# One-core decode block: the loads issued by GpSimd as single packets in place of SyncE's loads

## The chip, the core and the metric

The kernel runs on one core of a Trainium2 chip. The metric is device time in microseconds (us), the median of three runs. TensorE (PE) does the matmuls, VectorE (DVE) and ScalarE (ACT) the elementwise work, GpSimd (POOL) and SyncE (SP) little besides constants and transfers. Transfers between the chip's memory (DRAM) and the on-chip buffer run on the core's 16 DMA engines, whichever engine issues them.

## The reference

One token of width 640 goes through an attention block with a cached context and then a gated feed-forward block:

```python
B, Sq, D = 1, 1, 640
H, Sk, Dh = 32, 8192, 192
q = (layernorm(x) @ wq) per head
scores = einsum("bhqd,bhkd->bhqk", q, k_cache) * (Dh ** -0.5)
o = einsum("bhqk,bhkd->bhqd", softmax(scores), v_cache)
h = x + o @ wo
gate, up = layernorm(h) @ W_gate, layernorm(h) @ W_up      # F = 1536
out = h + (relu(gate) * up) @ W_down
```

All data are float32. Keys and values of 32 heads, 8192 positions and 192 features each are 403 MB; with the weights some 446 MB have to be read once.

## The kernel before

The host packs the inputs into matrices of 128 rows, one row for each partition, in the order in which they are used. The on-chip buffer holds three slots of 128 x 16320 floats, `slot_x`, `slot_y` and `slot_z` (`X`, `Y`, `Z` in the code). A load fills (most of) a slot: 128 rows of up to 65,280 bytes, one for each partition, eight for each DMA engine.

Heads are worked on in units (`pe_unit`): scores of one head from its keys (`pe_k`, L180), the values of the head before it (`pe_v`, L187), and the query and output projections on VectorE (`dve_d1`, `dve_wo`). A loop of `NTURN` = 10 turns handles three heads a turn. Each turn has five loads, `row_1` to `row_5`: `row_1` into X, `row_2` into Z, `row_3` into Y, `row_4` into X, `row_5` into Y. Ahead of the loop `row_p` goes into Y; behind it come the last head and the feed-forward weights in eleven smaller loads with `row_p` (`row_t1`, `row_t2a`, `row_t2b`, `row_t3`, `row_up`, `row_gate`, four pieces of `row_down`). That makes 61 loads.

Two families of semaphores set the order. `land[n]` (and `tl[...]` behind the loop) rises to 16 when load n has landed; PE and DVE wait for it. `free[n]` tells that the consumers are done with the part of a slot that load n filled; the issuer waits for it, takes 16 off `land[n]`, and issues the next load into that slot. `free[5]`, for instance, is set by DVE when its last instruction of `dve_wo` (L377) on `woc` in Y is done, and `row_3` goes into Y on that. In the kernel before all this is SP's program (`sync_program`); GpSimd's program (`pool_program`) writes a few constants at the start (`ones`, `pat`, `ident`) and is then done. At the end `fout` tells that the output `o4` is written; SP and ACT each store one half, and SP waits for both (`out_s`, `out_a`).

The kernel reserves 2048 bytes of each partition for descriptors of transfers that GpSimd issues (`dynamic_dma_scratch_size`); before the change nothing uses them.

Of the kernel before, what the change touches and what calls it, by code (L numbers as in the profile page):

```python
# [8 lines left out]
ET = mybir.EngineType  # L9

P, D, H, S, DH, F = 128, 640, 32, 8192, 192, 1536
# [7 lines left out]
NTURN = (H - 2) // 3  # L19
SCALE = DH ** -0.5  # L20
EPS = 1e-5
DG, FG = D // 4, F // 4

W_P = 14272
# [61 lines left out]
def build(nc, arrays):  # L86
# [31 lines left out]
    o4 = sb("o4", [P, DG])  # L118
# [14 lines left out]
    def wait(eng, s, n, sub=0, **kw):  # L133
        w = eng.wait_ge(s, n)  # L134
        if sub:
            w.then_inc(s, -sub)
        return w
# [37 lines left out]
    te = nc.tensor  # L175
# [37 lines left out]
    def pe_unit(kblk, vblk, rows, freed=None, freed_at=None, q_next=True):  # L213
        def landed(n):
            if n in rows:
                s, sub = rows[n]
                wait(te, s, 16, sub)

        wait(te, a2p, 1, 1)
        landed("k0")  # L220
        pe_k(kblk, 0)
        wait(te, a2p, 1, 1)
        pe_o()
        wait(te, a2p, 1, 1)
        pe_l()
        landed("k1")
        pe_k(kblk, 1)
        landed("v0")
        at = None if freed is None else (freed_at, freed)
        pe_v(vblk, 0, 8, inc_at=at)  # L230
        landed("v8")
        pe_v(vblk, 8, 24, inc_at=at)
        if q_next:
            wait(te, d2p, 2, 2)
            if freed is not None and freed_at < 24 and freed is not fin:
                te.sem_inc(freed, 1)
            pe_q()
        else:
            wait(te, d2p, 1, 1)
        pe_t()  # L240
        landed("v24")
        pe_v(vblk, 24, 32, last=p2a)

    def tensor_program():
        wait(te, cst_pe, 1, 1)
        wait(te, pre, 1, 1)
        op(te.matmul(pl[:, 0:1], ones, vec["s1"], start=True, stop=True), inc=p2d)
        wait(te, pre, 1, 1)
        op(te.matmul(pl[:, 0:1], ones, vec["s2"], start=True, stop=True), inc=p2d)
        wait(te, d2p, 1, 1)  # L250
        pe_q()
        wait(te, a2p, 1, 1)
        wait(te, land[5], 16)
        pe_k(kp, 0)
        pe_k(kp, 1)
        wait(te, d2p, 2, 2)
        pe_q()
        pe_t()
        with te.Fori(0, NTURN):
            pe_unit(ka, va, {"k0": (land[1], 0), "v8": (land[2], 0)}, free[1], 7)  # L260
            pe_unit(kb, vb, {"k1": (land[3], 0), "v24": (land[4], 0)}, free[3], 23)
            pe_unit(kc, vcc, {"v0": (land[5], 0)})
        pe_unit(kt, vt, {"k0": (tl["t1"], 16), "v8": (tl["t2a"], 16)}, fin, 7, q_next=False)
        wait(te, a2p, 1, 1)
        pe_o()
        wait(te, a2p, 1, 1)
        pe_l()
        wait(te, tl["t2b"], 16, 16)
        pe_v(vz, 0, 16)
        wait(te, d2p, 3, 3)  # L270
        for g in range(4):
            te.matmul(acc[Q(g), 0:DG], ones[Q(g), 0:32], xd[Q(g)].rearrange("p c j -> p (c j)"),
                      start=True, stop=False, tile_position=(32 * g, 32 * g))
        for g in range(4):
            te.matmul(acc[Q(g), 0:DG], ones[:, 0:32], accs[:, g * DG:(g + 1) * DG], start=False, stop=False)
        for g in range(4):
            r = slice(0, 64) if g < 2 else slice(64, P)
            te.matmul(acc[Q(g), 0:DG], ones[r, 0:32], accs[r, D + (g % 2) * DG:D + (g % 2 + 1) * DG],
                      start=False, stop=False)
        wait(te, tl["t3"], 16, 16)  # L280
        pe_v(vz, 16, 32, last=p2a)
        wait(te, a2p, 1, 1)
        pe_o()
        wait(te, d2p, 1, 1)
        for g in range(4):
            te.matmul(acc[Q(g), 0:DG], oc[:, 0:1].to_broadcast([P, 32]), woz[:, g * DG:(g + 1) * DG],
                      start=False, stop=False)
        for g in range(4):
            r = slice(0, 64) if g < 2 else slice(64, P)
            m = te.matmul(acc[Q(g), 0:DG], oc[r, 1:2].to_broadcast([64, 32]),  # L290
                          woz[r, D + (g % 2) * DG:D + (g % 2 + 1) * DG], start=False, stop=True)
        m.then_inc(p2a, 1)
        wait(te, a2p, 1, 1)
        op(te.matmul(pt[:, 0:1], ones, vec["hs1"], start=True, stop=True), inc=p2d)
        wait(te, d2p, 1, 1)
        op(te.matmul(od[:, 0:1], ones, vec["hs2"], start=True, stop=True), inc=p2d)
        wait(te, tl["up"], 16, 16)
        for j in range(DJ):
            for g in range(4):
                m = te.matmul(sc[Q(g), 0:FG], hc[:, j, :], up[:, j, g * FG:(g + 1) * FG],  # L300
                              start=(j == 0), stop=(j == DJ - 1))
        op(m, inc=p2a)
        wait(te, tl["gate"], 16, 16)
        for j in range(DJ):
            for g in range(4):
                m = te.matmul(sc[Q(g), 512:512 + FG], hc[:, j, :], gate[:, j, g * FG:(g + 1) * FG],
                              start=(j == 0), stop=(j == DJ - 1))
        op(m, inc=p2d)
        wait(te, d2p, 1, 1)
        wait(te, tl["d0"], 16, 16)  # L310
        for j in range(FJ):
            if j == 6:
                wait(te, tl["d1"], 16, 16)
            if j == 10:
                wait(te, tl["d2"], 16, 16)
            if j < FJ - 1:
                for g in range(4):
                    te.matmul(q_ps[Q(g), 0:DG], guT[:, j, :], down[:, j * D + g * DG:j * D + (g + 1) * DG],  # L318
                              start=(j == 0), stop=False)
            else:  # L320
                for half in range(2):
                    if half:
                        wait(te, tl["d3"], 16, 16)
                    for g in range(2 * half, 2 * half + 2):
                        m = te.matmul(q_ps[Q(g), 0:DG], guT[:, j, :], down[:, j * D + g * DG:j * D + (g + 1) * DG],  # L325
                                      start=False, stop=True)
        op(m, inc=p2d)
# [199 lines left out]
        po_.sem_inc(cst_pe, 1)  # L527
        po_.sem_inc(cst_ve, 1)

    sp = nc.sync  # L530

    def load(t, src, s):
        sp.dma_start(t, src).then_inc(s, 16)

    def sync_program():
        load(Y[:, 0:W_P], dram["row_p"], land[5])
        r1, r2, r3, r4, r5 = (dram[f"row_{i}"] for i in range(1, 6))
        load(X[:, 0:W_1], r1[0], land[1])
        load(Z[:, 0:W_2], r2[0], land[2])

        def turn(i):
            wait(sp, free[5], 1, 1)
            wait(sp, land[5], 16, 16)
            load(Y[:, 0:W_3], r3[i], land[3])
            wait(sp, free[1], 2, 2)
            wait(sp, land[1], 16, 16)
            load(X[:, 0:W_4], r4[i], land[4])
            wait(sp, free[3], 2, 2)
            wait(sp, land[3], 16, 16)
            load(Y[:, 0:W_5], r5[i], land[5])  # L550
            wait(sp, free[2], 1, 1)
            wait(sp, land[2], 16, 16)
            wait(sp, free[4], 1, 1)
            wait(sp, land[4], 16, 16)

        with sp.Fori(0, NTURN - 1) as i:
            turn(i)
            load(X[:, 0:W_1], r1[i + 1], land[1])
            load(Z[:, 0:W_2], r2[i + 1], land[2])
        turn(NTURN - 1)  # L560
        load(X[:, 0:W_T1], dram["row_t1"], tl["t1"])
        load(Z[:, 0:W_T2A], dram["row_t2a"], tl["t2a"])
        load(Z[:, W_T2A:W_T2A + W_T2B], dram["row_t2b"], tl["t2b"])
        wait(sp, free[5], 1, 1)
        wait(sp, land[5], 16, 16)
        load(Y[:, 0:W_T3], dram["row_t3"], tl["t3"])
        load(Y[:, W_T3:W_T3 + W_UP], dram["row_up"], tl["up"])
        wait(sp, fin, 1, 1)
        load(X[:, 0:W_UP], dram["row_gate"], tl["gate"])
        for n, (a, b) in enumerate(DOWN):  # L570
            load(X[:, W_UP + a:W_UP + b], dram["row_down"][:, a:b], tl[f"d{n}"])
        wait(sp, fout, 1)
        load(out[0, 0, 0:D // 2].rearrange("(g n) -> g n", g=2), o4[31:33, :], out_s)
        wait(sp, out_s, 16, 16)
        wait(sp, out_a, 16, 16)
        wait(sp, fout, 1, 1)

    programs = ((ET.PE, tensor_program), (ET.DVE, vector_program), (ET.Activation, scalar_program),
                (ET.Pool, pool_program), (ET.SP, sync_program))
    for e, _ in programs:  # L580
        nc.br(f"prog_{e.name}", engines=[e])
    for e, f in programs:
# [12 lines left out]
```

## Time and profile before

| | us |
|---|---|
| median of 3 runs | 1039.3 (1038.07 to 1039.48) |
| the profiled execution's own time | 1039.63 |
| its span, first to last instruction | 1038.3 |
| PE busy | 547.4 (53%) |
| DVE busy | 188.2 (18%) |
| POOL busy | 1.2 |
| time that the packets of SP's queue took, share of 16 engines | 99.4% |

The profile comes from one execution, 0.3 us above the median; 1.3 us of it lie outside the span. Busy shares of engines are averages over the span. The DMA share is the mean over the 16 DMA engines; a packet in the table of queues is one transfer of one engine as the profiler records it. An issue (SPq) is the instruction with which an engine starts a load; its time to landing runs from there to the last byte's semaphore.

### The profile page before, as it was taken

How to read it: one execution, taken by the hardware profiler on the slowest of the kernel's cores; microseconds unless marked ns; L12 is line 12 of the kernel's file. 1: busy time of each engine (PE TensorE's matmuls, PEld its weight loads, DVE VectorE, ACT ScalarE, POOL GpSimd, SP SyncE). 2: the span in 40 equal slices, each digit the busy share in tenths (PEclk: the TensorE clock that was granted, in tenths of full speed). 3: DMA queues.
4: the chain of work that ended last, by engine and by line, in shares of the span. 5: the costliest groups of instructions: out<-in, count | busy, mean ns of one | idle time of the engine just before them, and what ended most of it. 6: DMA issues, size and time to landing. Idle time of an engine off the chain costs nothing. (4 is left out here: it accounts for less than half of the span.)

```text
span 1038.3 us, 10306 instructions
## 1 busy us (share of the span) xinstructions
PE 547.4 (53%) x4492; PEld 176.3 (17%) x4492; DVE 188.2 (18%) x478; ACT 41.2 (4%) x137; POOL 1.2 (0%) x11
## 2 busy tenths in 40 slices
PE   0746446456363563654544546536465463564676
PEld 0211112112121120111111112112111121121123
DVE  1211221112122021221121220212221121220111
ACT  1000000000000000000000000000000000000010
POOL 0000000000000000000000000000000000000000
PEclk9876867768677677776787867867877778687787
DMA  9999999999999999999999999999999999999997
GB/s 402 441 432 425 434 435 431 445 420 435 435 439 433 425 438 436 440 427 432 435 435 426 433 438 431 444 426 433 433 438 438 420 438 436 438 432 425 432 427 326
DMA packets 8800, 446.07 MB, mean 430 GB/s; under 512 B 980, under 2 KB 1112, under 8 KB 1240
## 3 DMA queue, kind: packets, MB, share of 16 engines
q1 hardware_dynamic: 8788, 445.94, 99.4%
q8 instruction: 7, 0.11, 0.0%
q14 instruction: 1, 0.01, 0.0%
q10 hardware_dynamic: 4, 0.00, 0.0%
HBM read 445.94 MB, written 0.00 MB: 429 GB/s over the span
## 5 line engine op out<-in xcount | busy, mean ns | idle before, releaser
L180 PE MATMUL sc<-slot_x,qs 128*32 128x512 f32 x1008 | 150.9, 743 | 109.6 <-DMA slot_x<-row 99.9
L187 PE MATMUL po<-slot_y,p 128*2 128x384 f32 x1152 | 117.9, 562 | 80.2 <-DMA slot_y<-row 77.4
L187 PE MATMUL po<-slot_z,p 128*2 128x384 f32 x560 | 72.5, 671 | 91.7 <-DMA slot_z<-row 88.4
L180 PE MATMUL sc<-slot_y,qs 128*32 128x512 f32 x288 | 54.1, 913 | 83.0 <-DMA slot_y<-row 82.5
L187 PE MATMUL po<-slot_x,p 128*2 128x384 f32 x336 | 43.6, 651 | 86.1 <-DMA slot_x<-row 86.1
L373 DVE COPY oc<-od 128x2 f32<-128x2 f32 x32 | 5.1, 159 | 389.5 <-PE od L206 389.5
L385 DVE STREAM_TRANSPOSE st<-sc 128x512 f32<-128x512 f32 x64 | 45.7, 714 | 164.4 <-PE sc L180 164.4
L180 PEld LDWEIGHTS sc<-slot_x,qs 128*32 128x32 f32 x1008 | 35.4, 134 | 200.8 <-DMA slot_x<-row 106.3
L187 PEld LDWEIGHTS po<-slot_y,p 128*2 128x2 f32 x1152 | 29.1, 94 | 167.7 <-DMA slot_y<-row 86.5
L391 DVE TENSOR_REDUCE m<-pt 128x1 f32<-128x128 f32 x32 | 9.3, 292 | 162.6 <-PE pt L199 162.6
L187 PEld LDWEIGHTS po<-slot_z,p 128*2 128x2 f32 x560 | 15.0, 102 | 138.3 <-DMA slot_z<-row 95.6
L474 ACT COPY qs<-q_ps 128x96 f32<-128x96 f32 x32 | 7.7, 239 | 766.9 <-ACTq L134 766.9
L367 DVE SCALAR_TENSOR_TENSOR prod<-slot_y,xn,prod 128x192 f32<-128x192 f32 x88 | 36.9, 419 | 3.1
L180 PEld LDWEIGHTS sc<-slot_y,qs 128*32 128x32 f32 x288 | 11.4, 154 | 113.8 <-DMA slot_y<-row 83.4
L180 PE MATMUL sc<-slot_z,qs 128*32 128x512 f32 x240 | 27.6, 592 | 0.0
L187 PEld LDWEIGHTS po<-slot_x,p 128*2 128x2 f32 x336 | 8.6, 94 | 109.5 <-DMA slot_x<-row 88.0
L203 PEld LDWEIGHTS od<-mrl,ob 128*128 128x128 f32 x132 | 18.1, 199 | 34.2 <-issue 34.2
L478 ACT COPY ob<-po 128x384 f32<-128x384 f32 x32 | 15.3, 479 | 181.1 <-ACTq L134 181.1
L203 PE MATMUL od<-mrl,ob 128*128 128x1 f32 x132 | 20.8, 262 | 1.6 <-PEq L134 1.6
L194 PE MATMUL q_ps<-pat,prod 128*128 128x96 f32 x64 | 15.4, 323 | 8.5 <-PEq L134 8.5
L365 DVE TENSOR_SCALAR prod<-slot_y,xn 128x192 f32<-128x192 f32 x22 | 6.9, 315 | 65.4 <-DMA slot_y<-row 65.3
L376 DVE SCALAR_TENSOR_TENSOR accs<-slot_y,oc,accs 128x640 f32<-128x640 f32 x21 | 18.5, 879 | 0.0
(95 smaller groups left out, 248.6 us busy)
## 6 DMA issues: line engine op xcount, KB each, us to landing
slot_x<-row SPq DMA_DIRECT2D x10, 8160.0 KB, 26.9
slot_z<-row SPq DMA_DIRECT2D x10, 8160.0 KB, 45.8
slot_y<-row SPq DMA_DIRECT2D x10, 8160.0 KB, 24.7
slot_x<-row SPq DMA_DIRECT2D x10, 7680.0 KB, 35.6
slot_y<-row SPq DMA_DIRECT2D x10, 7584.0 KB, 27.1
slot_x<-row_t SPq DMA_DIRECT2D x1, 7680.0 KB, 25.2
slot_y<-row_p SPq DMA_DIRECT2D x1, 7136.0 KB, 19.6
slot_z<-row_t2a SPq DMA_DIRECT2D x1, 5088.0 KB, 36.9
```

The costliest lines, as they stand in the source:

```text
L180: m = te.matmul(sc[Q(g), half * 512:half * 512 + 512], qs[:, 32 * part:32 * part + 32], blk(half, part * 4 + g), start=(part == 0), stop=( ...
L187: m = te.matmul(po[32 * g:32 * g + 2, 0:PW], p[:, 2 * i:2 * i + 2], blk(i), start=(i < 4), stop=(i >= 28))
L194: te.matmul(q_ps[:, 0:96], prod[:, 0:P], pat[:, 0, :], start=True, stop=False)
L203: te.matmul(od[:, 0:1], ob[:, k * DH:k * DH + P], mrl[:, k:k + 1], start=(k == 0), stop=(k == 1))
L365: dv(ve.tensor_scalar(prod, w3[:, 0, :], xn[:, 0:1], None, op0=ALU.mult), w=first)
L367: dv(STT(prod, w3[:, j, :], xn[:, j:j + 1], prod, op0=ALU.mult, op1=ALU.add), w="self", inc=d2p if j == DJ - 1 else None)
L373: dv(ve.tensor_copy(oc, od[:, 0:2]), w=pd())
L376: dv(STT(accs[:, 0:D], w[:, 0:D], oc[:, 0:1], accs[:, 0:D], op0=ALU.mult, op1=ALU.add), w="self", inc=inc)
L385: return dv(ve.transpose(st[:, s], sc[:, s]), w=w)
L391: dv(ve.reduce_max(vec["m1"], pt[:, 0:P], axis=AX.X, negate=True), w=pd(), inc=d2a)
L474: op(ac.copy(qs, q_ps[:, 0:96]), inc=a2p)
L478: op(ac.copy(ob, po[:, 0:PW]), inc=a2p)
```

## The change

All 61 loads move from SP's program to GpSimd's. Each is issued with `single_packet`, which asks the software that writes GpSimd's descriptors to mark all of one engine's rows of a load as one packet. Where SP took 16 off a landing semaphore as part of its wait, GpSimd now waits and then runs an instruction of its own (`inc_swdge_sem`, mode "sub"), which keeps its books on its queue as well. PE therefore no longer takes 16 off the `tl` semaphores behind the loop; GpSimd does that at the very end, ten times, and only then sets `fin`, for which SP waits behind the two stores. GpSimd's constants are written behind its first three loads. SP keeps the store of its half of the output.

```diff
+SINGLE = True
...
-        wait(te, tl["t2b"], 16, 16)
+        wait(te, tl["t2b"], 16)
...
-    def load(t, src, s):
-        sp.dma_start(t, src).then_inc(s, 16)
-
-    def sync_program():
+    def load(t, src, s, **kw):
+        po_.dma_start(t, src, single_packet=SINGLE, **kw).then_inc(s, 16)
+
+    def settled(s):
+        wait(po_, s, 16)
+        po_.inc_swdge_sem([s], [16], mode="sub")
+
+    def load_program():
         load(Y[:, 0:W_P], dram["row_p"], land[5])
...
         load(X[:, 0:W_1], r1[0], land[1])
         load(Z[:, 0:W_2], r2[0], land[2])
+        pool_program()
 
         def turn(i):
-            wait(sp, free[5], 1, 1)
-            wait(sp, land[5], 16, 16)
+            wait(po_, free[5], 1, 1)
+            settled(land[5])
             load(Y[:, 0:W_3], r3[i], land[3])
...
-        with sp.Fori(0, NTURN - 1) as i:
+        with po_.Fori(0, NTURN - 1) as i:
             turn(i)
...
+        wait(po_, fout, 1)
+        for s in tl.values():
+            settled(s)
+        po_.sem_inc(fin, 1)
+
+    sp = nc.sync
+
+    def sync_program():
         wait(sp, fout, 1)
-        load(out[0, 0, 0:D // 2].rearrange("(g n) -> g n", g=2), o4[31:33, :], out_s)
+        sp.dma_start(out[0, 0, 0:D // 2].rearrange("(g n) -> g n", g=2), o4[31:33, :]).then_inc(out_s, 16)
         wait(sp, out_s, 16, 16)
         wait(sp, out_a, 16, 16)
+        wait(sp, fin, 1, 1)
         wait(sp, fout, 1, 1)
```

The first place is the loop. These are the rows of SP in one turn before (an ISA row is the wait and the computing of the address; the names in brackets are the semaphores waited for):

```order
L533 ISA [waits free5,land5]
L533 DMA slot_y<-row 128x16320
L533 ISA [waits free1,land1]
L533 DMA slot_x<-row 128x15360
L533 ISA [waits free3,land3]
L533 DMA slot_y<-row 128x15168
L533 ISA [waits free2,land2,free4,land4]
L533 DMA slot_x<-row 128x16320
L533 DMA slot_z<-row 128x16320
```

And these are the rows of POOL in one turn of the change, L536 being the instruction that takes 16 off and L532 the address and the load:

```order
L536 ISA [waits free5,land5]
L532 ISA
L532 DMA slot_y<-row 128x16320
L536 ISA [waits free1,land1]
L532 ISA
L532 DMA slot_x<-row 128x15360
L536 ISA [waits free3,land3]
L532 ISA
L532 DMA slot_y<-row 128x15168
L536 ISA [waits free2,land2]
L536 ISA [waits free4,land4]
```

Every load now has one or two more instructions between its wait and its issue, all on POOL's queue; the waits themselves and the order of the loads are the same.

The second place is the end of POOL's program, from the last load on (before, POOL has nothing there):

```order
L532 DMA slot_x<-row_down 128x320
L536 ISA [waits tl_t1,fout]
L536 ISA [waits tl_t2a]
L536 ISA [waits tl_t2b]
L536 ISA [waits tl_t3]
L536 ISA [waits tl_up]
L536 ISA [waits tl_gate]
L536 ISA [waits tl_d0]
L536 ISA [waits tl_d1]
L536 ISA [waits tl_d2]
L536 ISA [waits tl_d3]
```

Ten instructions come behind `fout`, beside the store of the output, and SP, behind its wait for the two stores, now waits for the end of them.

## Rows read from the trace of the kernel before

**Rows 1.** The page's first part: busy time, share of span, instructions.
```profile
span 1038.3 us, 10306 instructions
PE 547.4 (53%) x4492; PEld 176.3 (17%) x4492; DVE 188.2 (18%) x478; ACT 41.2 (4%) x137; POOL 1.2 (0%) x11
```

**Rows 2.** The page's DMA totals, and its queues (packets, MB, share of 16 engines).
```profile
DMA packets 8800, 446.07 MB, mean 430 GB/s; under 512 B 980, under 2 KB 1112, under 8 KB 1240
...
q1 hardware_dynamic: 8788, 445.94, 99.4%
q8 instruction: 7, 0.11, 0.0%
```

**Rows 3.** Who waited for whom: engine, line, releaser: total us, times, longest.
```profile
PE sc L180 <- DMA slot_x<-row: 99.9, 9, 11.5
...
PE po L187 <- DMA slot_z<-row: 88.4, 10, 9.4
...
PE po L187 <- DMA slot_x<-row: 86.1, 10, 9.1
...
PE sc L180 <- DMA slot_y<-row: 82.5, 10, 8.7
PE po L187 <- DMA slot_y<-row: 77.4, 10, 8.2
```

**Rows 4.** Rates by stretch: us, busy of each engine, PEclk, DMA share, GB/s.
```profile
100.00:900.00 800.00, 419.95 (x3407) 131.47 (x3399) 146.24 (x363) 28.62 (x103) 0.00 (x0) 0.76 1.00 433
...
1005.00:1022.00 17.00, 12.24 (x96) 4.79 (x100) 2.27 (x11) 1.08 (x4) 0.00 (x0) 0.63 1.01 432
...
1026.50:1030.00 3.50, 3.50 (x29) 1.41 (x21) 0.00 (x0) 0.00 (x0) 0.00 (x0) 0.51 1.01 426
```

**Rows 5.** DMA issues of the page: count, KB each, median us to landing.
```profile
slot_x<-row SPq DMA_DIRECT2D x10, 8160.0 KB, 26.9
slot_z<-row SPq DMA_DIRECT2D x10, 8160.0 KB, 45.8
slot_y<-row SPq DMA_DIRECT2D x10, 8160.0 KB, 24.7
slot_x<-row SPq DMA_DIRECT2D x10, 7680.0 KB, 35.6
slot_y<-row SPq DMA_DIRECT2D x10, 7584.0 KB, 27.1
...
slot_y<-row_p SPq DMA_DIRECT2D x1, 7136.0 KB, 19.6
```

**Rows 6.** The first turn's `row_3`, alone, by the same view.
```profile
slot_y<-row SPq DMA_DIRECT2D x1, 8160.0 KB, 23.7
```

**Rows 7.** Timeline of the start: start us, us, engine, line, operation.
```profile
0.31 0.10 POOL L590 MEMSET const-float32-0.0<- 128x1 f32 x1 [0.31 <-issue]
...
0.41 0.10 POOL L590 MEMSET const-uint8-127<- 128x1 uint8 x1
0.81 0.42 SPq L533 DMA_DIRECT2D slot_y<-row_p  x1
...
1.36 0.29 POOL L522 TENSOR_SCALAR_AFFINE_SELECT ident<-ones 128x128 f32<-128x128 f32 x1
...
1.60 0.25 POOL L525 MEMSET pat<- 128x16 f32 x4
```

**Rows 8.** Timeline of the second turn around the issue of `row_3`.
```profile
146.71 0.88 DVE L376 SCALAR_TENSOR_TENSOR accs<-slot_y,oc,accs 128x640 f32<-128x640 f32 x1
147.51 0.55 DVE L377 SCALAR_TENSOR_TENSOR accs<-slot_y,oc,accs 128x320 f32<-128x320 f32 x1
148.43 0.33 SPq L533 DMA_DIRECT2D slot_y<-row  x1
...
154.22 3.38 PE L187 MATMUL po<-slot_z,p 128*2 128x384 f32 x20 [9.26 <-DMA slot_z<-row]
```

**Rows 9.** Timeline of the end.
```profile
1026.02 5.13 PE L306 MATMUL sc<-slot_x,hc 128*32 128x384 f32 x40 [2.42 <-PEq L134]
...
1036.47 0.38 DVE L467 SCALAR_TENSOR_TENSOR o<-q_ps,hr,h 128x160 f32<-128x160 f32 x1 [3.83 <-PE q_ps L325]
1036.88 0.34 SPq L533 DMA_DIRECT2D out<-o  x1
```

**Rows 10.** The queues in the stretch of 2 us from 102 to 104.
```profile
q8 instruction: 1, 0.02, 3.2%
```

More of the change, by code (lines that the diff above doesn't have):

```diff
@@ L262, in tensor_program @@
             pe_unit(kc, vcc, {"v0": (land[5], 0)})
-        pe_unit(kt, vt, {"k0": (tl["t1"], 16), "v8": (tl["t2a"], 16)}, fin, 7, q_next=False)
+        pe_unit(kt, vt, {"k0": (tl["t1"], 0), "v8": (tl["t2a"], 0)}, fin, 7, q_next=False)
         wait(te, a2p, 1, 1)
@@ L279, in tensor_program @@
                       start=False, stop=False)
-        wait(te, tl["t3"], 16, 16)
+        wait(te, tl["t3"], 16)
         pe_v(vz, 16, 32, last=p2a)
@@ L296, in tensor_program @@
         op(te.matmul(od[:, 0:1], ones, vec["hs2"], start=True, stop=True), inc=p2d)
-        wait(te, tl["up"], 16, 16)
+        wait(te, tl["up"], 16)
         for j in range(DJ):
@@ L302, in tensor_program @@
         op(m, inc=p2a)
-        wait(te, tl["gate"], 16, 16)
+        wait(te, tl["gate"], 16)
         for j in range(DJ):
@@ L309, in tensor_program @@
         wait(te, d2p, 1, 1)
-        wait(te, tl["d0"], 16, 16)
+        wait(te, tl["d0"], 16)
         for j in range(FJ):
             if j == 6:
-                wait(te, tl["d1"], 16, 16)
+                wait(te, tl["d1"], 16)
             if j == 10:
-                wait(te, tl["d2"], 16, 16)
+                wait(te, tl["d2"], 16)
             if j < FJ - 1:
@@ L322, in tensor_program @@
                     if half:
-                        wait(te, tl["d3"], 16, 16)
+                        wait(te, tl["d3"], 16)
                     for g in range(2 * half, 2 * half + 2):
@@ L528, in pool_program @@
         po_.sem_inc(cst_ve, 1)
-    sp = nc.sync
-    def load(t, src, s):
-        sp.dma_start(t, src).then_inc(s, 16)
-    def sync_program():
+    def load(t, src, s, **kw):
[4 more added lines that the diff above has]
+    def load_program():
+        r1, r2, r3, r4, r5 = (dram[f"row_{i}"] for i in range(1, 6))
         load(Y[:, 0:W_P], dram["row_p"], land[5])
-        r1, r2, r3, r4, r5 = (dram[f"row_{i}"] for i in range(1, 6))
         load(X[:, 0:W_1], r1[0], land[1])
         load(Z[:, 0:W_2], r2[0], land[2])
+        pool_program()
         def turn(i):
-            wait(sp, free[5], 1, 1)
-            wait(sp, land[5], 16, 16)
+            wait(po_, free[5], 1, 1)
+            settled(land[5])
             load(Y[:, 0:W_3], r3[i], land[3])
-            wait(sp, free[1], 2, 2)
-            wait(sp, land[1], 16, 16)
+            wait(po_, free[1], 2, 2)
+            settled(land[1])
             load(X[:, 0:W_4], r4[i], land[4])
-            wait(sp, free[3], 2, 2)
-            wait(sp, land[3], 16, 16)
+            wait(po_, free[3], 2, 2)
+            settled(land[3])
             load(Y[:, 0:W_5], r5[i], land[5])
[L551 to L554, printed above, removed]
-        with sp.Fori(0, NTURN - 1) as i:
+            wait(po_, free[2], 1, 1)
+            settled(land[2])
+            wait(po_, free[4], 1, 1)
+            settled(land[4])
+        with po_.Fori(0, NTURN - 1) as i:
             turn(i)
@@ L563, in sync_program @@
         load(Z[:, W_T2A:W_T2A + W_T2B], dram["row_t2b"], tl["t2b"])
-        wait(sp, free[5], 1, 1)
-        wait(sp, land[5], 16, 16)
+        wait(po_, free[5], 1, 1)
+        settled(land[5])
         load(Y[:, 0:W_T3], dram["row_t3"], tl["t3"])
         load(Y[:, W_T3:W_T3 + W_UP], dram["row_up"], tl["up"])
-        wait(sp, fin, 1, 1)
+        wait(po_, fin, 1, 1)
         load(X[:, 0:W_UP], dram["row_gate"], tl["gate"])
@@ L571, in sync_program @@
             load(X[:, W_UP + a:W_UP + b], dram["row_down"][:, a:b], tl[f"d{n}"])
+        wait(po_, fout, 1)
[4 more added lines that the diff above has]
+    def sync_program():
         wait(sp, fout, 1)
-        load(out[0, 0, 0:D // 2].rearrange("(g n) -> g n", g=2), o4[31:33, :], out_s)
+        sp.dma_start(out[0, 0, 0:D // 2].rearrange("(g n) -> g n", g=2), o4[31:33, :]).then_inc(out_s, 16)
         wait(sp, out_s, 16, 16)
         wait(sp, out_a, 16, 16)
+        wait(sp, fin, 1, 1)
         wait(sp, fout, 1, 1)
     programs = ((ET.PE, tensor_program), (ET.DVE, vector_program), (ET.Activation, scalar_program),
-                (ET.Pool, pool_program), (ET.SP, sync_program))
+                (ET.Pool, load_program), (ET.SP, sync_program))
     for e, _ in programs:
```

## The prediction

> **What bounds the kernel now.** I read the page's engine shares first: no compute engine is busy for much more than half of the span, and POOL for 1.2 us [rows 1]. The transfers fill it instead: the packets of SP's queue take 99.4% of 16 engines' time, 446 MB in all [rows 2]. The waits say the same from the other side: ten times each, PE stands idle some 8 to 10 us for one of the five loads of a turn [rows 3]. So PE, DVE and ACT could all be somewhat later or earlier and nothing would change; the end moves with the last bytes. Next, the rate. Between 100 and 900 us, 433 GB/s flow at a DMA share of 1.00 [rows 4]. At that rate 446 MB take 1030 us; some 2 to 3 us lie ahead of the first bytes and 3 to 5 behind the last, and 1.3 outside the span.
>
> Whether a load is issued early enough is read from its time to landing less its own transfer. A load of 8160 KB is 8.36 MB, 19.3 us at 433 GB/s. The three such loads land 26.9, 45.8 and 24.7 us after their issue, the other two (7680 and 7584 KB, 18.2 and 17.9 us) after 35.6 and 27.1 [rows 5]. So they are issued 7.6, 26.5, 5.4, 17.4 and 9.2 us ahead of the moment at which their own bytes could start. The thinnest cover is that of `row_3`: 5.4 us in the median, 23.7 - 19.3 = 4.4 us in the first turn [rows 6]. The timeline shows its chain: DVE ends `dve_wo` at 148.06, SP issues at 148.43, and PE sees the load ahead of it, `row_2`, land at 154.22 [rows 8].
>
> **The change, part by part.**
>
> *The start.* SP issues `row_p` at 0.81 with an instruction of 0.42 us [rows 7]. It lands 19.6 us later, though 7.31 MB take 16.9 us at 433 GB/s, so 2.7 us are latency and ramp [rows 5, 4]. Nothing hides this. GpSimd's issue replaces SP's, and no row shows how long its software needs for a load. Lower end: no longer than SP, 0.42 us. Upper end: POOL starts its shortest instructions every 0.034 us (four from 0.31 to 0.41, [rows 7]); if each of the 128 rows of a load cost that much, 4.4 us. The ends lie a factor of ten apart and neither row is like it, so I take the geometric middle, 1.4 us, and so +1.0 us (0 to +4.0). The Trainium skill ("DMA: Bandwidth & Descriptors", Specifications) gives about 1 us to the first byte on GpSimd's path and 0.6 on SP's; no trace here has yet shown GpSimd's. By it this term would be +0.4, an estimate from that page, and the sum 0.6 lower. The constants behind the first three loads are wanted only when `row_p` has landed, some 20 us in, so they cost nothing; if they came later than that, they would count in full.
>
> *The stream.* Each of the 50 loads of the loop gets one or two instructions more between wait and issue, and the longer issue: +0.05 to +0.11 us for each taking of 16 (as much as POOL's short instructions, [rows 7]) and +1.0 us. What hides it is the load still under way. `row_3`, with 5.4 us of cover, needs at most the 2.7 us of latency that the first load shows; 2.7 us are left (1.7 in the first turn), against 1.2 wanted. So 0. If the cover goes, each microsecond too much is lost ten times. What is queued behind a late `row_3` on POOL are `row_4` and `row_5`, with 17.4 and 9.2 us of cover, so they follow without harm. The Trainium skill ("SBUF — State Buffer", SBUF: two separate sides) warns against just this: while VectorE runs certain instructions, GpSimd cannot write its descriptors, and its transfers wait. The longest DVE instruction there takes 0.88 us [rows 8]; by the rule `row_3` would be short by nothing, since 1.2 + 0.9 stays under 2.7, and by the trace as I read it also by nothing, so the sum is the same here; at a larger price it is the third rival below.
>
> *One packet for each engine.* A load is 128 rows and 16 completion writes (61 loads give 8784 of the queue's 8788 packets, 976 of the 980 small ones, [rows 2]). Marked as one packet, an engine's share has one boundary in place of nine; 61 x 8 = 488 boundaries go from each engine. Price of a boundary: the loop's rows, 63,590 bytes on average, flow at 433 GB/s, rows of 30,720 bytes (1005 to 1022, `row_up` and `row_gate`) at 432, rows of 15,360 bytes (1026.5 to 1030, the first piece of `row_down`) at 426 [rows 4]. As one row's time on one engine (bytes times 16 over the rate) that is 2350, 1138 and 577 ns. A straight line through the first and the second leaves 5 ns at zero bytes, through the first and the third 12 ns. Both are coarse, since the rates are whole numbers and the last stretch has only 3.5 us; I take 8 ns. So at most 488 x 8 ns = 3.9 us go (5.9 at 12 ns), and at least nothing, if the price is that of a row's new address at both ends, which stays. I cannot tell the two apart from these rows. The second seems nearer to what happens, since the row still starts in another partition, and I take a fifth: -0.8 us.
>
> *The end.* Behind `fout` SP's store takes from 1036.88 to the end of the span, 1.4 us [rows 9, 1]. Beside it POOL takes 16 off ten times. Four short POOL memsets need 0.25 us together, one of them some 0.1 alone [rows 7], so ten need 0.6 to 1.1 us, just under the store. With the hand-over by `fin` I put +0.2 us (0 to +1.5, if each is as long as the 0.29 us of POOL's select).
>
> **Sum:** +1.0 + 0 - 0.8 + 0.2 = +0.4 us. The profiled execution, 1039.63 us, is 0.3 above the median, which changes no term; on the median of 1039.3 the prediction is 1039.7 us.
>
> **The rivals.** What the measurement can tell from no change is about 0.2%, 2.1 us.
>
> *Boundaries were the whole overhead* (faster). All of the 3.9 to 5.9 us go: +1.2 - 3.9 to -5.9 makes 1034.6 to 1036.6, say 1035.5 us. For it speaks that short rows run slower at a full DMA share; against it that row starts and packets coincide in this trace. It decides from about 7 ns for each boundary on (3.3 / 488).
>
> *Each row costs more when software wrote its descriptor* (slower). If an engine has to fetch what SP's hardware handed to it, one more price of a boundary for each of 488 rows gives +3.9, with +1.2 about 1044.4 us; all loads end with the slowest engine, so one engine slower by 1% costs 10 us, 1050. The DMA share of 1.00 speaks for it: every nanosecond on a row counts. Against it: rows this long leave 2.4 us to fetch the next. The Trainium skill ("DMA: Bandwidth & Descriptors", Latency and other measured facts) says that DMA engines 7 and 15 are usually slower than the others with GpSimd's loads, with a cause that it calls a guess; no run here shows it yet. It decides from 1 us (0.1%) on one engine.
>
> *`row_3` is issued too late* (slower). At the upper end, an issue of 4.4 us, it is 4.0 + 0.1 later and the cover short by 1.4 us; ten turns cost 14 us and the start 4, so about 1057. It decides from some 2.7 us of extra issue. The DVE rule above would be a way to get there.
>
> *Fetches of instructions wait longer* (slower). They share the engines: seven packets in the run [rows 2], the one near 102 us taking 3.2% of 2 us on 16 engines, so 1 us on one engine [rows 10]. If an engine changes queues only between packets, a fetch now waits for up to 8 rows, 19.3 us, where it waited for one, 2.4. PE stands 8 to 10 us for loads in each unit [rows 3], so three such fetches in the loop could cost up to 3 x 10 us, 1070. Against it: PE spends those idle times waiting for loads anyway, so a fetch asked for well ahead is not missed, and ahead of its matmuls at 1026, near the end, it still has 2.4 us of idle time [rows 9].
>
> **How the numbers follow.** Within 0.2% as forecast: 0.45. All boundaries gone: 0.20. Rows dearer: 0.20. Late issue: 0.07, late fetches 0.03, and the start and the end together above 2.1 us with no gain 0.05, all slower. So faster 0.20, same 0.45, slower 0.35. The range goes from 1035.5, which leaves out the half of the first rival below it (0.09), to 1047, which leaves out the late issue, the fetches and a slow single engine (0.11); the likeliest case by itself lies between 1037.3 and 1041.4.
>
> **What would show it.** `row_p` lands about 1 us later in the span than before. The steady rate stays at 433 GB/s; 434 to 435 means that boundaries were the overhead, 431 or less that rows got dearer. `row_3` lands some 23 to 24 us after its issue, with no gap in the DMA slices; a gap each turn means a late issue. The end keeps about 1.4 us behind `fout`. I am wrong if the rate moves by more than 0.2%, or if POOL's issue takes longer than its cover.

## The result and the profile after

The change made the kernel slower by 0.4%: 1042.6 us against 1038.4 us, medians of nine runs each, ratio 1.004 with a 95% interval of 1.0031 to 1.0049. The single runs spread from 1041.0 to 1045.5, those of the kernel before from 1037.9 to 1039.8. The 4.1 us lie inside the range that was given, but above what the likeliest case (no change beyond 2.1 us) allowed. The two profiled executions took 1039.63 and 1042.32 us, so the traces below show 2.7 us of the 4.1.

First the page of the kernel after, its totals and queues; they answer to [rows 1, 2]:

```profile
span 1040.7 us, 10308 instructions
...
DMA packets 8641, 446.08 MB, mean 429 GB/s; under 512 B 980, under 2 KB 984, under 8 KB 1080
...
q0 software_dynamic: 8624, 445.94, 99.2%
```

All loads now run on the queue of GpSimd's software, which is nearly as full as SP's was (99.2% against 99.4%). The steady stretch of the same kernel, to hold against the first of [rows 4]:

```profile
100.00:900.00 800.00, 425.94 (x3419) 132.90 (x3419) 145.55 (x362) 28.63 (x103) 22.20 (x42) 0.74 1.00 433
```

433 GB/s at a DMA share of 1.00, to the digit what it was. So a row costs neither less nor more, and the 4 us are not spread over the loads. They lie at the start, in the first turn, behind the loop and at the end. The start, in the timeline (answers to [rows 7]):

```profile
1.46 0.67 POOL L532 DMA_DIRECT2D slot_y<-row_p  x1 [0.82 <-POOLq L603]
...
21.64 0.16 DVE L430 TENSOR_REDUCE s<-slot_y 128x1 f32<-128x5 f32 x1 [16.81 <-DMA slot_y<-row_p]
```

DVE's first use of `row_p` stood at 20.49 before:

```profile
20.49 0.16 DVE L429 TENSOR_REDUCE s<-slot_y 128x1 f32<-128x5 f32 x1 [17.80 <-DMA slot_y<-row_p]
```

So everything begins 1.15 us later. The first turn: the moment at which `row_3` is issued, at which PE goes on with `row_2` (slot_z) and at which it goes on with `row_3` (slot_y). Before:

```profile
55.84 0.34 SPq L533 DMA_DIRECT2D slot_y<-row  x1
60.05 4.70 PE L187 MATMUL po<-slot_z,p 128*2 128x384 f32 x32 [7.69 <-DMA slot_z<-row]
...
79.61 5.19 PE L180 MATMUL sc<-slot_y,qs 128*32 128x512 f32 x24 [8.73 <-DMA slot_y<-row]
```

After:

```profile
57.52 0.58 POOL L532 DMA_DIRECT2D slot_y<-row  x1 [53.30 <-DMA slot_y<-row_p]
61.21 4.61 PE L188 MATMUL po<-slot_z,p 128*2 128x384 f32 x32 [7.84 <-DMA slot_z<-row]
...
81.82 4.56 PE L181 MATMUL sc<-slot_y,qs 128*32 128x512 f32 x24 [9.89 <-DMA slot_y<-row]
```

From `row_2` to `row_3` 19.56 us pass on PE before, close to one load's transfer of 19.3, and 20.61 after, 1.05 us more. The packets tell what happens there (which packets follow each other on one DMA engine is worked out from their times). After, the engines end their shares of `row_2` one by one from 58.8 us on, the first only 1.3 us behind the issue of `row_3` at 57.52; the first packets of `row_3` come 1.4 to 3.8 us behind that issue, and single engines have nothing to do for up to 2.5 us. Before, the first engine ends 1.9 us behind the issue, and only one waits, for 0.8 us. The completion writes of each load in the two traces tell the whole run (the last of 16 writes of a load, after less before, worked out from the trace):

```
row_p +1.18   row_1 +1.17   row_2 +1.12   row_3 of turn 1 +2.34
turn 3, row_3 +2.20   turn 6, row_3 +2.20   turn 10, row_5 +2.20
row_t1 +3.57   row_up +3.58   row_gate +2.55   last piece of row_down +2.54
```

Two steps, one at the start and one at the first `row_3`, and then a flat line for nine turns. Behind the loop the changed kernel loses another 1.4 us at `row_t1`, and the kernel before 1.0 at `row_gate`. Each time one DMA engine that is 1.4 to 1.8 us behind the first one already carries a fetch of instructions of 16 KB (1.1 us at 973.6 after, 1.0 us at 1020.4 before), and the load ends with that engine. Seven such fetches stand in every trace; what they cost depends on the engine that each falls on.

Of the 2.5 us at the last piece 1.7 reach the store of the output (1036.88 before, 1038.58 after): PE's matmuls on `row_gate` took 5.13 us before [rows 9], at a granted clock of 0.51 of full speed between 1026.5 and 1030 us [rows 4] (about its lower level, 1.2 GHz), and 3.43 us after, at 1.00 (2.4 GHz). PE had been idle for 2.4 us ahead of them before and for 2.7 after. The end (answers to [rows 9]), and with it GpSimd's takings of 16, by the view of one line:

```profile
1038.16 0.38 DVE L468 SCALAR_TENSOR_TENSOR o<-q_ps,hr,h 128x160 f32<-128x160 f32 x1 [4.81 <-PE q_ps L326]
1038.58 0.34 SPq L585 DMA_DIRECT2D out<-o  x1
```

```profile
L536 POOLq INC_SWDGE_SEM  x61: 150/162/188, 56.6 to 1040.4; - x61
```

From the store's issue to the end of the span are 2.1 us, where [rows 9, 1] have 1.4: the last of ten takings starts at 1040.4, 1.8 us after the store. They follow each other every 0.2 us. The time outside the span also grew, from 1.4 us (median of the runs before) to 2.1 (1.7 in the three kernels below that have the same end).

### The profile page after: what moved, and what is told of

Same layout as the page of the kernel before. It is cut to its first block, busy times and chain, and to the rows that moved or that the text cites. A ratio compares the mean times of both kernels' runs of the same rounds, so it can differ in the third digit from the quotient of the medians.

```text
span 1040.7 us, 10308 instructions
## 1 busy us (share of the span) xinstructions
PE 545.8 (52%) x4492; PEld 175.4 (17%) x4492; DVE 188.2 (18%) x478; ACT 41.3 (4%) x137; POOL 33.6 (3%) x72
## 3 DMA queue, kind: packets, MB, share of 16 engines
q0 software_dynamic: 8624, 445.94, 99.2%
## 5 line engine op out<-in xcount | busy, mean ns | idle before, releaser
L188 PE MATMUL po<-slot_y,p 128*2 128x384 f32 x1152 | 120.7, 573 | 79.6 <-DMA slot_y<-row 75.2
L181 PE MATMUL sc<-slot_y,qs 128*32 128x512 f32 x288 | 56.2, 945 | 83.1 <-DMA slot_y<-row 82.5
L532 POOL DMA_DIRECT2D slot_y<-row x20 | 10.7, 533 | 661.7 <-DMA slot_y<-row 345.9
L532 POOL DMA_DIRECT2D slot_x<-row x20 | 10.6, 531 | 246.0 <-DMA slot_x<-row 246.0
```

The lines of the kernel that those rows point to most:

```text
L181: m = te.matmul(sc[Q(g), half * 512:half * 512 + 512], qs[:, 32 * part:32 * part + 32], blk(half, part * 4 + g), start=(part == 0), stop=( ...
L188: m = te.matmul(po[32 * g:32 * g + 2, 0:PW], p[:, 2 * i:2 * i + 2], blk(i), start=(i < 4), stop=(i >= 28))
L532: po_.dma_start(t, src, single_packet=SINGLE, **kw).then_inc(s, 16)
```

## The experiments

All ratios are to the kernel before, run on the same chip beside them (1038.1 to 1038.4 us). Theory A says three fixed places: the late start, the late `row_3` of the first turn, the takings of 16 behind `fout`. Its rivals are in the expectations.

**The request for one packet, taken back.**

```diff
-SINGLE = True
+SINGLE = False
```

> The loads stay on GpSimd, the request for one packet is taken back. Theory A (three fixed places: the start +1.2 us, row_3 of the first turn late by +1.1, the taking of 16 behind fout +0.7; nothing for each row): no difference to the changed kernel, 1042.5 within 0.8 us, steady rows as long as with the flag. Theory B (one long packet costs: rows or the fetches of instructions that wait behind it): most of the 4.1 us come back, 1039 to 1040.

Measured: 1042.4 us, 1.0037 (1.0025 to 1.0049). The page has the same 8624 packets on q0 and the steady stretch the same 433 GB/s. The flag is worth nothing that can be seen here, in either direction (the two times could differ by some 1.5 us unseen; the steady rate shows nothing); the 4 us come from the move to GpSimd. In its profiled run `row_3` of the first turn is late too, by more:

```profile
56.74 0.57 POOL L532 DMA_DIRECT2D slot_y<-row  x1 [52.53 <-DMA slot_y<-row_p]
60.96 4.23 PE L188 MATMUL po<-slot_z,p 128*2 128x384 f32 x32 [8.38 <-DMA slot_z<-row]
...
82.47 5.35 PE L181 MATMUL sc<-slot_y,qs 128*32 128x512 f32 x24 [11.16 <-DMA slot_y<-row]
```

21.51 us between the two waits' ends, so 2 us lost, more than in the first trace. The loss differs from run to run, and so does the time.

**`dve_wo` ahead of `dve_d1`**, so that `free[5]` comes earlier.

```diff
...
-            dve_unit(woc, wqb, freed_wo=free[5])
+            dve_unit(woc, wqb, freed_wo=free[5], wo_first=True)   # dve_wo and its free[5], then dve_d1
```

> The changed kernel, with VectorE's dve_wo ahead of dve_d1 in the first unit of each turn, so that row_3 is asked for some 2.1 us earlier. Theory A: row_3 of the first turn is no longer late, the shift of the landings against the kernel before stays at 1.1 us instead of rising to 2.3, time 1041.4. If the 1.1 us come from something else (slower first rows, a fetch), the landings still step up and the time stays at 1042.5.

Measured: 1040.0 us, 1.0015 (1.0007 to 1.0024), and the runs now lie between 1039.7 and 1040.9. Its timeline:

```profile
53.88 0.57 POOL L534 DMA_DIRECT2D slot_y<-row  x1 [49.67 <-DMA slot_y<-row_p]
60.81 4.92 PE L188 MATMUL po<-slot_z,p 128*2 128x384 f32 x32 [9.04 <-DMA slot_z<-row]
...
80.41 5.34 PE L181 MATMUL sc<-slot_y,qs 128*32 128x512 f32 x24 [8.56 <-DMA slot_y<-row]
```

19.60 us: the step is gone. The gain, 2.5 us in the median, is more than the 1.05 read from one trace. Part of it need not be `row_3`: this profile loses 0.3 us at `row_t1`, the one of the changed kernel 1.4. With one profile of each kernel the two can't be told apart in the median.

**Six of the ten takings of 16 ahead of `fout`.**

```diff
         wait(te, tl["gate"], 16)
+        te.sem_inc(mid, 1)
...
-        wait(po_, fout, 1)
-        for s in tl.values():
+        wait(po_, mid, 1, 1)
+        for n, s in tl.items():
+            if n == "d0":
+                wait(po_, fout, 1)
             settled(s)
```

> The changed kernel, with six of the ten takings of 16 done before fout, as soon as TensorE is past its wait for row_gate; four are left beside the store. Theory A: the stretch from the store's issue to the end of the span falls from 2.1 us to the 1.4 of the kernel before, time 1041.9. If the end is longer because of the store or of something on GpSimd's queue as such, it stays at 2.1 and 1042.5.

Measured: 1040.8 us, 1.0034 (1.002 to 1.0047), six runs from 1039.9 to 1044.9; nothing is done about `row_3` in it, so the time by itself is inconclusive. The profiled execution is the fastest of the six, and in it `row_3` is not late: it is issued at 56.17, PE goes on with `row_2` at 61.14 and with `row_3` 19.28 us later; at `row_t1` 1.1 us are lost. The end decides: the store is issued at 1037.21 and the span ends at 1038.7, 1.5 us, and the time outside the span is 1.2 us in the median instead of 2.1.

```profile
80.42 5.35 PE L181 MATMUL sc<-slot_y,qs 128*32 128x512 f32 x24 [8.15 <-DMA slot_y<-row]
...
1037.21 0.34 SPq L588 DMA_DIRECT2D out<-o  x1
```

**Both together.** The two edits above.

> Both edits at once, dve_wo first and six takings of 16 ahead of fout. Theory A (three fixed places): what is left over the kernel before is the late start, so 1038.3 + 1.1 = 1039.4, and no run far above the others, as there is no late row_3 any more. Theory C (GpSimd's path costs something in every turn as well, hidden in the spread): stays at 1040 or above.

Measured: 1039.0 us, 1.0003 (0.9994 to 1.0012), all of eleven runs within 1 us. Against the first edit alone the end is worth 1.0 us, by medians 0.5 in the span and 0.4 outside (in the two traces the stretch behind the store is 0.6 us shorter).

**The control: `dve_wo` first, with SyncE's loads.**

> The kernel before, SyncE's loads, with dve_wo ahead of dve_d1 in the first unit. Theory A: row_3 is in time already, so no difference, 1038.3 within 0.5. If the edit is a gain in itself (row_3 late in the kernel before, too), 1037 to 1037.8, and the gain seen with GpSimd's loads is partly not the repair of lateness.

Measured: 1038.3 us, 0.9997 (0.9988 to 1.0006). The edit gains nothing by itself; with GpSimd's loads it repaired something that hardly costs anything with SyncE's.

**A late start alone, with SyncE's loads.**

```diff
+        po_.sem_inc(cst_sp, 1)        # end of pool_program
...
+        wait(sp, cst_sp, 1, 1)        # start of sync_program
         load(Y[:, 0:W_P], dram["row_p"], land[5])
```

> The kernel before, SyncE's loads kept, but its first load held until GpSimd's constants are written, about 1.4 us later. If a late start counts in full and no more: 1038.4 + 1.4 = 1039.8, all landings shifted by 1.4 us. If a late start is what makes row_3 of the first turn late, the landings step up there as well and the time is some 1041.

Measured: 1040.3 us, 1.002 (1.0011 to 1.0029), so +1.9 in the median; the landings are shifted by 1.3 to 1.4 us from the first load to the last of the loop, with no step at `row_3`. In this profile a late start counts in full, and does not by itself make `row_3` late. (The half microsecond more than 1.4 isn't explained.)

**SyncE's first three loads, GpSimd's others.** SP issues `row_p`, `row_1` and `row_2` of the first turn; GpSimd's first turn is written out ahead of the loop and takes those three semaphores back by plain waits.

```diff
+        for t, n, k, w in ((Y, "row_p", 5, W_P), (X, "row_1", 1, W_1), (Z, "row_2", 2, W_2)):
+            sp.dma_start(t[:, 0:w], dram[n] if n == "row_p" else dram[n][0]).then_inc(land[k], 16)
...
```

> The changed kernel, with SyncE issuing the first three loads as in the kernel before; all others stay on GpSimd. Theory A: first landing back at 20.0 us in the span, row_3 of the first turn still late by about 1 us, the end as in the changed kernel: 1042.5 - 1.1 = 1041.4. If the late start is the cause of the late row_3: 1040.

Measured: 1041.2 us, 1.0027 (1.0015 to 1.004), near the 1041.4 of theory A, but six runs spread from 1039.5 to 1042.9, so this one alone does not decide. Its profile misses what theory A expected of `row_3`: the first one is not late, PE goes on with it at 79.57 where it did at 79.61 before. In this kernel the first `row_3` stands in another queue than `row_2` and runs beside its end, so the trace is no repetition of the case. What this execution loses is 1.55 us at `row_t1` and the end.

```profile
79.57 5.35 PE L181 MATMUL sc<-slot_y,qs 128*32 128x512 f32 x24 [5.46 <-DMA slot_y<-row]
```

**All three edits**, 58 of 61 loads still on GpSimd.

> All three edits: SyncE's first three loads, dve_wo first, six takings of 16 early; the other 58 loads on GpSimd. Theory A: nothing is left of the difference, 1038.3 within 0.5. Theory C: 1039 or above although start, row_3 and end are mended.

Measured: 1038.1 us, 0.9998 (0.9989 to 1.0007). Nothing is left. From here backwards the edits are worth: start 0.9 (1039.0 - 1038.1), end 1.0 (1040.0 - 1039.0), `dve_wo` first 2.5 (1042.5 - 1040.0). That these make the whole of it, 4.4 for the 4.1 measured, is so because the last version is level with the kernel before. `dve_wo` first is worth 1.8 where the end is mended already (1040.8 - 1039.0) and 2.1 with SyncE's first three loads, the end's 1.0 taken off (1041.2 - 1.0 - 1038.1). In the profiles a late first `row_3` stands in two of the four kernels without that edit and in none of the three with it; at `row_t1` the four lose 0.3 to 1.55 us (the one that loses 0.3 has lost 0.6 just ahead of it, at `row_5`), the three 0.3 to 0.45. No version beats the kernel before.

**How much cover `row_3` has.** Idle memsets on DVE ahead of `dve_wo`, in the first unit of each turn; the eight take 4.05 us in the timeline, from the first to the last, the sixteen 8.25.

```diff
         dve_mp()
+        for _ in range(hold):                       # 8 or 16 in the first unit of a turn, else 0
+            dv(ve.memset(gu, 0.0), w="self")
```

> The kernel before, SyncE's loads, with eight idle VectorE memsets (some 0.4 us each, 3.5 us in all) ahead of dve_wo in the first unit of each turn, so that row_3 is asked for 3.5 us later; nothing of GpSimd. If the cover is the 5.4 us of the prediction less the 2.7 us of latency, each turn loses 0.8 us and the time is about 1046. If only the engine that ends row_2 last counts, some 2 us behind the first, the loop's turns lose nothing and the first turn up to 1 us: 1039 to 1040.

> The same with sixteen memsets, 7 us later. By the first reading each turn loses 4.3 us, 1081; by the second 2.6 to 3.5 us, 1065 to 1073. If a late row_3 cost nothing with SyncE's loads, 1038.4.

> GpSimd's loads, with SyncE's first three and six takings of 16 early but without dve_wo first, and with the eight memsets in each turn. If GpSimd's longer way from the wait to the first bytes (1 to 2.5 us more than SyncE's) is what made row_3 late, each turn now loses 1 to 2 us: 1048 to 1058, against 1039 to 1040 with SyncE's loads. If the first turn's lateness came from something else, as with SyncE's, 1040 to 1042.

Measured: 1053.3 us with eight and SyncE (1.0145, 1.0128 to 1.0161), 1091.8 with sixteen (1.0517, 1.0499 to 1.0534), 1058.9 with eight and GpSimd (1.0199, 1.0182 to 1.0216). The landings show what a turn loses. From the landing of `row_5` in turn 1 to that in turn 10 the nine turns take 845.0 us without memsets, 856.9 with eight and 889.7 with sixteen: 1.3 us a turn for the first eight, 3.65 for the second. So SyncE's `row_3` has 4.05 - 1.3 = 2.7 us to spare in these turns, and beyond that a delay is lost nearly whole. That is the first reading, 5.4 less 2.7. It gave 1046 and 1081 because it put eight memsets at 3.5 us; with 4.05 it gives 10 x (4.05 - 2.7) = 13.5 us, 1051.6, and with 8.25 it gives 55.5 us, 1093.6. The second reading is refuted. In the first turn eight memsets cost 1.9 us, so there some 2.2 us are to spare.

With GpSimd's loads (859.3 us for the nine turns) each of these turns loses 0.3 us more than with SyncE's, the first turn 1.5 more, and `row_t1` 1.2 (the two profiled executions are 4.3 us apart, the medians 5.6). So in these two traces GpSimd's loads do cost something in every turn, as theory C has it, but only where the cover is gone. The timeline of the second turn shows the longer way to the issue:

```profile
154.69 0.55 DVE L379 SCALAR_TENSOR_TENSOR accs<-slot_y,oc,accs 128x320 f32<-128x320 f32 x1
156.27 0.53 POOL L537 DMA_DIRECT2D slot_y<-row  x1 [43.60 <-DMA slot_y<-row]
```

From the end of `dve_wo` at 155.24 to the issue are 1.03 us. With SP they are 0.37 [rows 8]. Without memsets the same stretch is 1.00 us in each of turns 2 to 9 of the changed kernel, and 0.38 in the kernel before.

## Why the prediction was right or wrong

**What bounds the kernel** was right: the transfers, at a rate that the change did not touch. So was the warning that a start and an end lie open and that `row_3` has the thinnest cover.

**The start** (+1.0, range 0 to +4.0) was right in its size, +1.15 in the trace and 0.9 to 1.3 by the runs with and without it, but in part by luck. The guessed instruction of 1.4 us is 0.67 us for the first load, 0.53 for the others, 0.25 more than SP's 0.42; more than half of the 1.15 is that it starts at 1.46, where SP's starts at 0.81, which no term had; and the first packet comes 1.4 us behind the issue, where it came 1.0 behind SP's.

**The stream** (0) is the step that failed, in the first turn. The mechanism was named, as the third rival, but it was given 0.07 and priced as ten late turns at an issue of 4.4 us; it was one late turn at an issue of 0.58. For the loop's other turns the working was right, not only its result: 2.7 us to spare with SP, as added up, of which GpSimd's longer way takes 0.6, and the landings stay flat. The first turn had been seen to be the thinnest, 4.4 us [rows 6], and was passed over with "1.7 left" against 1.2 wanted. What failed there is the 2.7 us that a load was taken to need at most behind its issue, from the landing of the first load, which met an idle queue. With leads from the issue to `row_2`'s end on PE of 3.7 and 4.2 us (57.52 to 61.21 and 56.74 to 60.96 above) GpSimd's first `row_3` took 20.61 and 21.51 us from there in place of 19.3; with 5.0 us, in the run with six early takings, it took 19.28, and every later turn of the kernels without memsets, where the lead is 4.7 us or more, took 19.3 too. With SP's lead of 4.2 (55.84 to 60.05) it took 19.56. A load's landing is that of its slowest DMA engine, and the engines end `row_2` over some 2 us; so a cover that is read from landings is that much too long for the engine that is done first.

**One packet** (-0.8) was wrong in its small way: 0. The price of a row stays with the row; 433 GB/s before and after, and with the flag off. That also closes the first rival (all boundaries gone) and the second (rows dearer). The Trainium skill ("DMA: Bandwidth & Descriptors", Latency and other measured facts) has engines 7 and 15 usually slower with GpSimd's loads; here the landings, which end with the slowest engine, stay at +2.20 us over seven turns (693 us), so no engine falls behind by even a thousandth. The Trainium skill's rule on DVE and descriptors ("SBUF — State Buffer", SBUF: two separate sides) is not tested here: all issues of whole slots take 530 to 577 ns, but beside them DVE runs reductions (with `dve_wo` first also `SCALAR_TENSOR_TENSOR`), and no run puts other instructions there on purpose.

**The end** (+0.2) was mis-sized: +1.0. Ten takings of 16 are 0.2 us apart, not 0.06 to 0.11 like memsets; that makes 2.0 us beside a store of 1.4, so 0.7 in the trace, and the rest lies outside the span.

**Late fetches of instructions**, as the rival had them, were not seen: a fetch of 16 KB takes 0.9 to 1.1 us of one DMA engine after and 0.9 to 1.3 before, and the flag changes neither time nor rate. But no term had the time of the fetches themselves. Where one falls on an engine that is behind already, the load ends later by up to 1.55 us; that happened at `row_t1` in all the profiles with GpSimd's loads (0.3 us and more) and in none with SyncE's, which lost up to 1.0 us at `row_gate` instead. Why it is so is open.

The sum was +0.4 and should have been +0.9 + 2.5 + 0 + 1.0 by the edits, in the prediction's order of terms, where the 2.5 are not `row_3` alone for certain. That 4.1 us still lie in the range is owed to its width.

## What to carry to other kernels

A kernel that keeps its DMA engines full is not safe against a slower issuer: look for the one load with the shortest lead, in the first pass of the loop above all, and move up the instruction that frees its slot; that took back 2.5 of the 4.1 us here. A cover read as "time to landing less transfer" has to pay for the whole way from wait to first bytes, on the DMA engine that is done first, and a delay put in on purpose measures what is left. One trace of each kernel may differ by a microsecond for reasons that have nothing to do with the change, so compare the landings one by one, to the last. Work that is new behind the last output counts in full once it is longer than the store beside it, so do it earlier.

## What the runs showed of the hardware

GpSimd's `inc_swdge_sem` takes 0.15 to 0.19 us and repeats every 0.2. An issue of a 128-row load takes GpSimd 0.53 us (SP 0.33), and comes 1.0 us after the end of the work it waits for (SP 0.37). The request for a single packet changed nothing that the profile or the time shows for rows of 57 to 65 KB. On an idle queue the first packet of a load comes 1.4 us behind GpSimd's issue and 1.0 behind SP's. A fetch of instructions takes 1 us from one DMA engine, and the engine stays behind the others through the loop. In the first turn single first packets of `row_3` came up to 3.8 us behind GpSimd's issue (4.6 with the flag off); behind SP's one came after 3.5 us in the kernel before, but all within 2.0 us in the run with sixteen memsets, where all engines were idle. Why is not settled.
